# Unread products, seeds and a load moved in the start-up of a Fourier mixing and gated convolution kernel

## The chip, the cores and the metric

The kernel runs on one core of a Trainium2 chip. The metric is the device time of one execution in microseconds (us), as the median of several runs. A core has engines that run side by side, each with its own queue in program order: TensorE (PE, with PEld for its weight loads), VectorE (DVE), ScalarE (ACT), GpSimd (POOL) and SyncE (SP), which here only issues DMA transfers. ACT and POOL issue transfers too.

## The reference, cut to what matters

```python
X = np.fft.fft(x, axis=1)            # x: 8 x 3136 x 256, float32
x = np.fft.fft(X, axis=2).real
h = np.maximum(x @ w_in, 0.0)        # w_in: 256 x 1024, float64
conv_out = sum(conv_w[k] * hp[:, k:k + S, :] for k in range(3))   # hp: h with a row of zeros at both ends
gate = 1.0 / (1.0 + np.exp(-conv_out))
out = (h * gate) @ w_out             # w_out: 1024 x 256, float64
```

The weights come as float64; the kernel makes float32 of them with integer and float operations on DVE (`narrow`, L617).

## The kernel before, in words

The first transform runs along the 3136 rows. The kernel folds x by symmetry (`fold_ops`, L142, on DVE, with small copies on POOL and scalings on ACT), and multiplies the folds with tables of cosines and sines on PE (`units`, L344): an odd table `tab4` (loaded at L280, partly mirrored by ACT at L309) and an even one `tab2` (L260). The results are `pt` and `qt`, `PQ[b]` in the code. The second transform, along the 256 features, isn't done by itself: its matrix `dm` is multiplied once with w_in, which gives G (`blocks(i)`, L752, eight matmul records of 256 columns for quarter i of w_in, and two copies by ACT) and a short vector `ge` (`column(i)`, L763, eight records of one column). One feature needs extra care: a row `er` is put together on POOL (L454, L455) from `qt`'s last row, which a transfer fetches (L463), then stored and spread over all partitions (L470, L573).

Then come 256 steps (batch, chunk of rows, 128 of the 1024 columns of w_in), in a pipeline written out by hand at L1051:

- `seed` (L786, ACT) writes the share of `er` times `ge` into a PSUM bank `pa` (two such banks);
- `products` (L794, PE) makes `pb` from `qt` and G (one bank) and adds `pt` times G to `pa`;
- `copies` (L807, ACT) takes `pb` out, `combine` (L815, DVE) adds, subtracts and clips at zero, which gives h;
- `first_tap` (L821, ACT), `middle` (L825, an adding transfer from POOL) and `last_tap` (L830, DVE) are the convolution, `sigmoid` (L845) and `gate` (L853 POOL, L854 DVE) follow, and `mm2` multiplies with w_out five steps later.

Other work is hung into the steps with `at(cycle, place, function)`; within a step the places come in the order first, act, dve, pool, load, pe. A step uses 128 columns, so steps 0 and 1 need only the first quarter of w_in, steps 2 and 3 the second. The transform of the next batch is spread over the steps of this one. The order on each engine is that of the program; nothing is rearranged later.

Before the steps stands the start-up: load w_in's first quarter and x of batch 0 (two halves, `load_ops(0, 0)` and `load_ops(0, 1)`; each half is one load, L119, and four gathers issued by POOL, L132; the second half also has three loads of single rows, L126, issued by ACT), then make float32 of the taps and of w_in's first quarter (`w4[0]`, done by L654), fold the first half, `blocks(0)` and `column(0)`, fold the second half, and transform. `keep_on` (L892) issues products of the folds `w` that nobody reads: two before `blocks(0)`, two after `column(0)`. A product of 512 columns is two matmul records in the trace. The buffer of x's second half is reused by batch 1's first half, whose loads (`load_ops(1, 0)`) stand after the copy of `er`'s spread row (L948). w_in's second quarter is made float32 ahead of the seeds (its three parts: `power` on DVE and ACT, L631 and L633; `product`, L645 and L646; `value`, L639 and L654). `column(1)` and `blocks(1)` follow after step 0's products.

Of the kernel before, what the change touches and what calls it, by code (L numbers as in the profile page):

```python
# [9 lines left out]
F32 = mybir.dt.float32  # L10
# [27 lines left out]
def kernel(  # L38
# [10 lines left out]
    nc = tc.nc  # L49
    B, S, D = x.shape  # L50
    F = moe_w_in.shape[1]
    P = 128
    M = S // 2
    Q4 = S // 4
    NP = Q4 // NQ
# [26 lines left out]
    psa = ctx.enter_context(tc.tile_pool(name="psa", bufs=2, space=PSUM))  # L82
    psb = ctx.enter_context(tc.tile_pool(name="psb", bufs=1, space=PSUM))
# [8 lines left out]
    def mm(o, l, r, start, stop):  # L92
        nc.tensor.matmul(o, l, r, start=start, stop=stop, skip_group_check=True)  # L93

    def spare():

        return pso.tile([P, 2, D], F32, name="po", tag="po").rearrange("p a d -> p (a d)")
# [4 lines left out]
    xh, wt, ea = {}, {}, {}  # L102
# [7 lines left out]
    def load_ops(b, h, eng, other=None, held=False):  # L110


        def plain():
            t = xp.tile([P, 8, 2, D], F32, name="xh", tag="xh")
            xh[b, h] = t
            if held:

                nc.gpsimd.memset(t[0:1, 0, 0, 0:1], 0.0)
            eng.dma_start(out=t[0:NP, 0:4], in_=bass.AP(  # L119
                tensor=x.tensor, offset=x.offset + (b * S + 1 + 2 * h) * D,  # L120
                ap=[[HQ * D, NP], [Q4 * D, 4], [1, 2 * D]]))

        def zero():
            t = xh[b, h]
            for s0, n, r in ((0, 4, 0), (4, 3, 1), (7, 1, 0)):
                (other or eng).dma_start(out=t[NP:KR, s0:s0 + n], in_=bass.AP(  # L126
                    tensor=x.tensor, offset=x.offset + (b * S + r * Q4) * D,
                    ap=[[D, 1], [Q4 * D, n], [0, 2], [1, D]]))

        def mirrored(m):  # L130
            def f():
                nc.gpsimd.indirect_dma_start(  # L132
                    out=xh[b, h][0:NP, 7 - m].rearrange("p q d -> p (q d)"),
                    out_offset=None,
                    in_=bass.AP(tensor=x.tensor, offset=x.offset,
                                ap=[[2 * D, B * S // 2], [1, 2 * D]]),
                    in_offset=bass.IndirectOffsetOnAxis(ap=idx[0:NP, 0:1], axis=0),
                    element_offset=(b * S + (4 - m) * Q4 - HO + 2 * (1 - h)) * D)
            return f
        return [plain] + [zero] * h + [mirrored(m) for m in range(4)]  # L140
# [150 lines left out]
    def load_turn(eng):  # L291

        for s in range(2):
            for i in range(2):
                eng.dma_start(out=turn[i:NP:2, s].unsqueeze(2), in_=bass.AP(
                    tensor=dft_seq.tensor, offset=dft_seq.offset + ((2 + s) * NQ + HQ * i) * HE,
                    ap=[[4 * NQ * HE, NP // 2], [2 * HE, 2], [1, 1]]))

    def mend_row(par, half):

        for st in range(2):
            row = tabs[0][96:NP, st, HQ - 1] if par == 0 else tabs[1][96:NP, st, 1]
            act(row, row, AF.Copy, scale=half[96:NP])
# [353 lines left out]
    class Weight:  # L657
# [19 lines left out]
        def narrow(self, c0, c1):  # L677
# [13 lines left out]
    win = [pqp.tile([P, NK], F32, name="win", tag=tag)[:, 0:F].rearrange("p (i t n) -> p i t n", i=2, t=2)  # L691
           for tag in ("pt", "qt")]
# [5 lines left out]
    w4 = [win[i // 2][:, i % 2] for i in range(4)]  # L698
    raws = [None, None]

    def raw_in(i):
        def f(sh):
            if i % 2 == 0:
                raws[i // 2] = wp.tile([P, 2, *sh[1:]], I32, name="raw", tag="w%d" % (i // 2))
            return raws[i // 2][:, i % 2]
        return f

    w_in = [Weight(w4[i], moe_w_in[:, i * N4:(i + 1) * N4].rearrange("(t p) n -> p t n", p=P), raw_in(i))
            for i in range(4)]
# [17 lines left out]
    for f in load_ops(0, 0, nc.sync):  # L727
        f()
    load_turn(nc.scalar)
    for f in load_ops(0, 1, nc.sync, nc.scalar, True):  # L730
        f()

    act(first_use, low, AF.Sigmoid)
# [18 lines left out]
    def blocks(i):  # L752

        w = w4[i]
        for g in range(2):
            p = spare()
            for t in range(2):
                mm(p[:, 0:N4], dm[:, t, g, :], w[:, t], t == 0, t == 1)
            nc.scalar.copy(out=G[:, g, i * N4:(i + 1) * N4], in_=p[:, 0:N4])
        if i > 1:  # L760
            column(i)

    def column(i):  # L763

        w, p = w4[i], spare()
        for m in range(NF // 4):
            for t in range(2):
                mm(p[:, m:m + 1], w[:, t, m * P:(m + 1) * P], dm[:, t, 1, P - 1:P], t == 0, t == 1)
        nc.scalar.copy(out=ge[:, i * NF // 4:(i + 1) * NF // 4], in_=p[:, 0:NF // 4])
# [4 lines left out]
    hs, gs, pa, pb, po, nb = {}, {}, {}, {}, {}, {}  # L774

    def cut(s):
        b, c, f = s
        ch = chunks[c]
        return ch, ch.k1 - ch.k0, slice(f * P, (f + 1) * P)

    def seed(s):

        b, c, f = s
        ch, n, fs = cut(s)
        pa[s] = psa.tile([P, 512], F32, name="pa", tag="pa")
        act(pa[s][:, 0:n], eb[b, c], AF.Copy, scale=ge[:, f:f + 1])  # L786
# [7 lines left out]
    def products(s):  # L794
        b, c, f = s
        ch, n, fs = cut(s)
        pb[s] = psb.tile([P, 512], F32, name="pb", tag="pb")
        mm(pb[s][:, 0:n], G[0:P - 1, 1, fs], PQ[b][1][0:P - 1, ch.k0:ch.k1], True, True)
        mm(pa[s][:, 0:n], G[:, 0, fs], PQ[b][0][:, ch.k0:ch.k1], False, True)

    def copies(s):

        ch, n, fs = cut(s)
        p = pb.pop(s)
        nb[s] = nbp.tile([P, 2, HN], F32, name="nb", tag="nb")
        for i, cols in enumerate((ch.fcols, ch.cols)):
            act(nb[s][:, i, cols], p[:, cols], AF.Copy, scale=-1.0 if i else 1.0)  # L807
# [79 lines left out]
        gs.pop(s)  # L887


    idle = psb.tile([P, 512], F32, name="pb", tag="pb")  # L890

    def keep_on(banks):  # L892

        for p in banks:
            mm(p.rearrange("p (s q d) -> p s q d", s=2, q=2), wt[0][1][0:NP, 1, 0], wt[0][1][0:NP, 0:2, 0:2],
               True, True)

    begin, us, row, flip, store = units(0)
    begin()
# [3 lines left out]
    ops, _, pres = fold_ops(0)  # L903

    def folds(h):
        n = len(ops) // 2
        for j in range(n * h, n * h + n):
            if j in pres:
                pres[j]()
            ops[j]()  # L910
# [2 lines left out]
    w_out = Weight(wout, moe_w_out.rearrange("(c p) o -> p c o", p=P),  # L913
                   lambda sh: xp.tile(sh, I32, name="raw", tag="xh"))
    w_out.load(nc.sync)
    keep_on([idle] * 2)
    blocks(0)
    column(0)
    keep_on([psa.tile([P, 512], F32, name="pa", tag="pa") for _ in range(2)])
    mend_row(1, half)  # L920
    mirror_tables()
    folds(1)
    mend_row(0, half)
    for i in range(2):
        for u in odds:
            u.part(i)
# [17 lines left out]
    n = chunks[0].k1  # L944
    p = psd.tile([P, 512], F32, name="pd", tag="pd")
    mm(p[:, 0:n], one, er[0][:, 0:n], True, True)
    eb[0, 0] = ebp.tile([P, HN], F32, name="eb", tag="eb")[:, 0:n]
    nc.scalar.copy(out=eb[0, 0], in_=p[:, 0:n])  # L948
    for f in load_ops(1, 0, nc.sync):
        f()  # L950
    room = left[:, NF // 2:].rearrange("p f i -> p (f i)").bitcast(I32)
    for f in w_in[1].parts(0, 2, room):
        f()
    steps = [(b, c, f) for b in range(B) for c in range(len(chunks)) for f in range(NF)]
    per = len(chunks) * NF
    side = {}
# [2 lines left out]
    def at(cycle, where, fn):  # L959
        side.setdefault((cycle, where), []).append(fn)  # L960
# [2 lines left out]
        at((0, 0, 1, 3)[i], "pe", lambda i=i: blocks(i))  # L963

    early, *rest = w_in[2].parts(0, 2, room)
    for fn in rest:
        at(0, "dve", fn)
    for cycle, w_, c in ((1, w_in[3], 0), (3, w_out, 0), (5, w_out, 2), (7, w_out, 4), (9, w_out, 6)):
# [29 lines left out]
    for b in range(1, B):  # L998
# [4 lines left out]
        n = per * b - (2 if b == 1 else 3) - c0  # L1003
# [12 lines left out]
    for b in range(1, B):  # L1016
        ops, singles, pres = fold_ops(b)
        c0, n = ends[b - 1], ends[b] - ends[b - 1]
# [4 lines left out]
        else:  # L1023
            if b == 2:
                c0, n = c0 + 3, n - 3
# [16 lines left out]
    n = len(steps)  # L1042
    row_of(steps[0])
    seed(steps[0])
    seed(steps[1])
    products(steps[0])
    copies(steps[0])
    early()
    column(1)
    blocks(1)  # L1050
    for t in range(n + LAG):  # L1051
        def run(where):
            for fn in side.get((t, where), []):
# [97 lines left out]
```

## Time and profile before

| | us |
|---|---|
| median of 3 runs | 1169.77 (1169.37 to 1169.94) |
| profiled execution | 1170.58 |
| its span, first to last instruction | 1168.8 |
| PE busy | 1136.6 (97%) |
| DVE busy | 975.2 (83%) |
| ACT busy | 943.2 (81%) |
| POOL busy | 607.8 (52%) |

The mean granted TensorE clock of the span is 0.997. A row of the order of time gives the start, the length, the engine, the line of the kernel, the operation, what it writes and reads (partitions x elements), how many were merged, and in brackets how long the engine was idle before and what ended that. A product shows the line of its helper, L93; the tiles tell products apart: `pb<-w` and `pa<-w` the unread ones, `po<-win,dm` the blocks, `po<-dm,win` the column, `po<-tab,..` the transforms, `pd<-er,one` the spread of the row, `pb<-qt,G` and `pa<-pt,G` those of a step. A name with q, as SPq, is the engine's queue of DMA issues. A row of busy time by stretches gives from and to, the length, then for PE, PEld, DVE, ACT and POOL the busy time with the number of instructions, then the granted clock, the mean busy share of the 16 DMA engines and GB/s.

### The profile page before, as it was taken

What the parts mean: (1) busy time and instruction counts of PE and PEld (TensorE: products, weight loads), DVE (VectorE), ACT (ScalarE), POOL (GpSimd) and SP (SyncE); (2) the same over time, 40 slices, a digit from 0 to 9 for tenths busy, and PEclk for the clock granted to TensorE, in tenths of its full rate; (3) what the DMA queues carried; (4) which work ended last, traced back from release to release, by engine and by line L of the source; (5) the groups of instructions that cost most, each with busy time, mean ns of one, the idle gap of its engine ahead of it and who ended that gap; (6) DMA issues with size and microseconds to landing.
All of it is one profiled execution on the core that took longest, in us unless ns stands there. A gap on an engine that the chain in (4) does not pass through costs nothing.

```text
span 1168.8 us, 15881 instructions
## 1 busy us (share of the span) xinstructions
PE 1136.6 (97%) x4810; PEld 888.5 (76%) x4810; DVE 975.2 (83%) x1448; ACT 943.2 (81%) x1939; POOL 607.8 (52%) x738
## 2 busy tenths in 40 slices
PE   3999999999999999999999999999999999999998
PEld 2766787778777777777777777777778777777777
DVE  7699989998788879898887888879787778788885
ACT  2598878888788879888887888888887888898885
POOL 6256545656466464646455464655344344444443
PEclk9899999999999999999999999999999999999999
DMA  9677896776677676767675666855665656666654
GB/s 240 165 112 161 173 152 148 165 162 153 132 148 169 136 180 133 168 115 177 142 168 127 147 133 139 183 122 122 136 120 102 125 122 142 131 130 128 125 117 105
DMA packets 106200, 168.15 MB, mean 144 GB/s; under 512 B 31275, under 2 KB 61241, under 8 KB 106115
## 3 DMA queue, kind: packets, MB, share of 16 engines
q0 software_dynamic: 42160, 115.87, 51.7%
q1 hardware_dynamic: 63183, 51.11, 15.9%
q8 instruction: 38, 0.62, 0.2%
q14 instruction: 47, 0.39, 0.1%
q10 hardware_dynamic: 772, 0.16, 0.1%
HBM read 38.40 MB, written 25.74 MB: 55 GB/s over the span
## 4 chain that ended last, share of the span: by engine, by line
PE 79%; ACT 5%; DVE 4%; issue 2%; DMA 0%; DVEq 0%; ACTq 0%
PE po L93 49%; PE pb L93 12%; PE pa L93 12%; PE pd L93 6%; DVE g L830 1%; ACT nb L807 1%; ACT g L845 1%; ACT os L878 1%; ACT pa L786 0%; DVE g L854 0%; DMA out_dram<-os 0%; ACT g L821 0%; DVE h L815 0%; DVE xh L168 0%; DVE xh L157 0%
## 5 line engine op out<-in xcount | busy, mean ns | idle before, releaser
L93 PE MATMUL po<-wout,g 128*128 128x256 f32 x3072 | 706.7, 379 | 5.4 <-DVE g L854 4.7
L93 PEld LDWEIGHTS po<-wout,g 128*128 128x128 f32 x3072 | 580.4, 190 | 151.2 <-issue 19.5
L825 POOL DMA_DIRECT2D g<-h x256 | 228.0, 890 | 465.6 <-ACT g L821 291.8
L845 ACT ACTIVATE g<-g,cw 128x385 f32<-128x385 f32 (+2 forms) x512 | 292.4, 625 | 67.2 <-DVE g L830 66.2
L853 POOL TENSOR_TENSOR g<-g,h 128x385 f32<-128x385 f32 (+1 forms) x256 | 299.1, 1169 | 44.4 <-ACT g L845 42.8
L807 ACT ACTIVATE nb<-pb 128x386 f32<-128x386 f32 (+3 forms) x512 | 227.4, 499 | 110.0 <-PE pb L93 109.2
L815 DVE CUSTOM_DVE_ANT_0 h<-pa,nb 128x386 f32<-128x386 f32 (+3 forms) x512 | 264.4, 556 | 32.0 <-POOL h L792 19.3
L830 DVE SCALAR_TENSOR_TENSOR g<-h,cw,g 128x770 f32<-128x770 f32 (+1 forms) x256 | 282.5, 1104 | 0.0
L821 ACT ACTIVATE g<-h,cw 128x770 f32<-128x770 f32 (+1 forms) x256 | 244.6, 955 | 0.0
L93 PE MATMUL pb<-qt,G 127*128 127x387 f32 (+2 forms) x512 | 214.4, 500 | 1.8 <-ACT nb L807 1.8
L93 PE MATMUL pa<-pt,G 128*128 128x387 f32 (+2 forms) x512 | 212.0, 495 | 1.7 <-ACT pa L786 1.7
L854 DVE TENSOR_TENSOR g<-g,h 128x385 f32<-128x385 f32 (+1 forms) x256 | 190.1, 743 | 24.6 <-ACT g L845 24.5
L786 ACT ACTIVATE pa<-eb,ge 128x387 f32<-128x387 f32 (+2 forms) x256 | 155.5, 608 | 1.6 <-DVE h L815 1.2
L93 PEld LDWEIGHTS pa<-pt,G 128*128 128x128 f32 x512 | 96.9, 190 | 76.1 <-issue 18.2
L132 POOL DMA_INDIRECT xh<-in_x_dram,idx x64 | 90.5, 1413 | 19.4 <-issue 11.6
L93 PEld LDWEIGHTS pb<-qt,G 127*128 127x128 f32 x512 | 91.2, 191 | 9.4 <-ACT nb L807 4.0
L93 PE MATMUL pd<-tab,w 98*128 98x197 f32 (+2 forms) x448 | 97.7, 317 | 0.2 <-DVE as L419 0.2
L93 PEld LDWEIGHTS pd<-tab,w 98*128 98x128 f32 (+1 forms) x448 | 81.9, 191 | 9.5 <-ACT pa L786 0.6
L878 ACT COPY os<-po 128x256 f32<-128x256 f32 x196 | 57.4, 394 | 6.5 <-PE po L93 6.5
L168 DVE TENSOR_TENSOR xh<-xh 98x1024 f32<-98x1024 f32 (+1 forms) x32 | 48.7, 1522 | 0.1
L157 DVE TENSOR_TENSOR xh<-xh 98x1020 f32<-98x1020 f32 (+1 forms) x32 | 46.1, 1445 | 0.0
L392 DVE TENSOR_TENSOR as<-as,pd 128x196 f32<-128x196 f32 x14 | 5.0, 359 | 37.0 <-ACT as L388 37.0
(143 smaller groups left out, 452.9 us busy)
## 6 DMA issues: line engine op xcount, KB each, us to landing
g<-h POOLq DMA_DIRECT2D x192, 385.0 KB, 4.1
g<-h POOLq DMA_DIRECT2D x64, 416.0 KB, 4.2
out_dram<-os SPq DMA_DIRECT2D x96, 256.0 KB
xh<-in_x_dram SPq DMA_DIRECT2D x16, 784.0 KB
eb<-ed SPq DMA_DIRECT2D x16, 193.5 KB
raw<-in_moe_w_in_dram SPq DMA_DIRECT2D x4, 512.0 KB
raw<-in_moe_w_out_dram SPq DMA_DIRECT2D x1, 2048.0 KB
eb<-ed SPq DMA_DIRECT2D x8, 209.0 KB
```

The lines of the kernel that those rows point to most:

```text
L93: nc.tensor.matmul(o, l, r, start=start, stop=stop, skip_group_check=True)
L132: nc.gpsimd.indirect_dma_start(out=xh[b, h][0:NP, 7 - m].rearrange("p q d -> p (q d)"), out_offset=None, in_=bass.AP(tensor=x.tensor, offs ...
L786: act(pa[s][:, 0:n], eb[b, c], AF.Copy, scale=ge[:, f:f + 1])
L807: act(nb[s][:, i, cols], p[:, cols], AF.Copy, scale=-1.0 if i else 1.0)
L815: nc.vector._custom_dve(TENSOR_ADD_SAT, out=to, in0=a[:, cols], in1=c[:, i, cols], s0=BIG, s1=0.0)
L821: act(gs[s], hs[s][:, 0:n], AF.Copy, scale=cw[:, 0, s[2]:s[2] + 1])
L825: nc.gpsimd.dma_start(out=gs[s], in_=hs[s][:, 1:1 + n], accum_op=ALU.add)
L830: stt(out=g, in0=h[:, k:k + n], scalar=cw[:, k, f:f + 1], in1=g, op0=ALU.mult, op1=ALU.add)
L845: act(gs[s][:, c], gs[s][:, c], AF.Sigmoid, scale=cw[:, 1, s[2]:s[2] + 1])
L853: gt(g[:, p], g[:, p], h[:, p], op=ALU.mult)
L854: vt(g[:, v], g[:, v], h[:, v], op=ALU.mult)
L878: nc.scalar.copy(out=osb[:, j % 2], in_=pt[:, j % 2])
```

## The change

The three single-row loads of batch 0 go from ACT's queue to SP's. The unread products of the folds `w` are gone; in their place stand nine of w_in's first quarter with itself, ahead of all folds: one into each `pa` bank, seven into `pb`. Batch 1's first half of x is loaded right after the folds of batch 0, ahead of its transform. The seeds of steps 0 and 1 go ahead of the second quarter's float32 parts, and `column(1)` and `blocks(1)` go into step 0's place "first", which is behind step 1's products and copies. On ACT that puts the two seeds ahead of L633, and step 1's copies ahead of the column's and blocks' copies. On POOL the four gathers stand ahead of L454, on SP the load ahead of L470.

```diff
-    for f in load_ops(0, 1, nc.sync, nc.scalar, True):
+    for f in load_ops(0, 1, nc.sync, None, True):
         f()
...
-    idle = psb.tile([P, 512], F32, name="pb", tag="pb")
-
-    def keep_on(banks):
-
-        for p in banks:
-            mm(p.rearrange("p (s q d) -> p s q d", s=2, q=2), wt[0][1][0:NP, 1, 0], wt[0][1][0:NP, 0:2, 0:2],
-               True, True)
+    for pool, tag, n in ((psa, "pa", 1), (psa, "pa", 1), (psb, "pb", 7)):
+        p = pool.tile([P, 512], F32, name=tag, tag=tag)
+        for _ in range(n):
+            mm(p, w4[0][:, 0, 0:P], win[0][:, 0].rearrange("p t n -> p (t n)"), True, True)
...
     w_out.load(nc.sync)
-    keep_on([idle] * 2)
     blocks(0)
     column(0)
-    keep_on([psa.tile([P, 512], F32, name="pa", tag="pa") for _ in range(2)])
     mend_row(1, half)
     mirror_tables()
     folds(1)
     mend_row(0, half)
+    for f in load_ops(1, 0, nc.sync):
+        f()
...
-    for f in load_ops(1, 0, nc.sync):
-        f()
     room = left[:, NF // 2:].rearrange("p f i -> p (f i)").bitcast(I32)
-    for f in w_in[1].parts(0, 2, room):
-        f()
...
+    at(0, "first", lambda: column(1))
+    at(0, "first", lambda: blocks(1))
...
     seed(steps[0])
     seed(steps[1])
+    for f in w_in[1].parts(0, 2, room):
+        f()
     products(steps[0])
     copies(steps[0])
     early()
-    column(1)
-    blocks(1)
```

## The prediction

> **What bounds the kernel now.** I read the page first, then the busy time by stretches, then the order of time in the first 60 us.
>
> ```profile
> span 1168.8 us, 15881 instructions
> ## 1 busy us (share of the span) xinstructions
> PE 1136.6 (97%) x4810; PEld 888.5 (76%) x4810; DVE 975.2 (83%) x1448; ACT 943.2 (81%) x1939; POOL 607.8 (52%) x738
> ```
> ```profile
> 0.00:20.00 20.00, 1.10 (x3) 1.00 (x4) 14.11 (x29) 1.66 (x4) 15.71 (x33) 1.00 0.90 225
> 20.00:45.00 25.00, 24.54 (x124) 18.71 (x122) 18.66 (x36) 12.47 (x32) 8.66 (x14) 1.00 0.68 205
> ...
> 70.00:100.00 30.00, 27.66 (x112) 20.63 (x111) 29.79 (x47) 24.85 (x52) 13.84 (x24) 1.00 0.60 117
> ...
> 150.00:200.00 50.00, 50.00 (x228) 39.83 (x227) 44.14 (x74) 37.69 (x78) 24.75 (x31) 1.00 0.78 157
> ```
>
> In the second answer the first bracketed pair after a stretch's length is PE, then weight loads, DVE, ACT, POOL; then the granted clock, DMA share and GB/s. PE is the bound: 50.00 of 50.00 us in 150 to 200. Of its 32.2 idle us (1168.8 - 1136.6), 18.9 lie before 20. In 70 to 100 DVE is full (29.79 of 30) and PE is not. So whatever brings all three engines to step 2 earlier is kept to the end; PE alone early is worth nothing. No part of the change reaches past about 60 us, except by that shift.
>
> **Part 1: the first 29 us.**
>
> ```profile
> 6.26 0.97 POOL L132 DMA_INDIRECT xh<-in_x_dram,idx  x1 [0.30 <-issue]
> ...
> 8.67 0.69 DVE L654 SCALAR_TENSOR_TENSOR win<-raw,win 128x512 f32<-128x512 f32 x1
> ...
> 11.50 0.17 DVE L717 TENSOR_TENSOR small<-cw 128x8 f32<-128x8 f32 x1 [2.14 <-ACT cw L715]
> ...
> 12.51 2.34 DVE L157 TENSOR_TENSOR xh<-xh 98x1020 f32<-98x1020 f32 x2
> ...
> 17.70 1.22 SPq L260 DMA_DIRECT2D tab<-dft_seq_dram  x2
> ...
> 19.49 3.78 PE L93 MATMUL pb<-w 98*128 98x512 f32 x4 [13.42 <-POOL w L179]
> ...
> 23.06 3.33 PE L93 MATMUL po<-win,dm 128*128 128x256 f32 x8
> ...
> 26.23 0.95 PE L93 MATMUL po<-dm,win 128*128 128x1 f32 x8
> ...
> 27.04 1.96 PE L93 MATMUL pa<-w 98*128 98x512 f32 x4
> ...
> 28.23 1.20 ACT L309 ACTIVATE tab<-tab 99x196 f32<-99x196 f32 x4
> ...
> 29.17 0.86 PE L93 MATMUL po<-tab,h 98*128 98x197 f32 x4
> ...
> 29.40 0.66 POOL L202 COPY ea<-xh 99x4 f32<-99x4 f32 x1
> ```
> ```profile
> xh<-in_x_dram,idx POOLq DMA_INDIRECT x1, 6.0
> ```
> ```profile
> SPq L670 <- DMA dm<-dft_dim_dram: 0.9, 1, 0.9
> ```
> ```profile
> tab<-dft_seq_dram SPq DMA_DIRECT2D x2, 589.5 KB
> ```
> ```profile
> DMA packets 175, 0.91 MB, mean 226 GB/s; under 512 B 24, under 2 KB 32, under 8 KB 175
> ```
> ```profile
> DMA packets 1173, 2.32 MB, mean 387 GB/s; under 512 B 39, under 2 KB 39, under 8 KB 1173
> ```
>
> The last two rows are all DMA from 20 to 24 and from 27 to 33.
>
> *The three row loads off ACT.* DVE's wait of 2.14 us for ACT goes. The second fold needs the fourth gather (issued 6.26, landing 6.0 later: 12.26); it began at 12.51 + 1.17 = 13.7. So the folds gain 1.3 of the 2.1 us: done at about 28.8, not 30.1. SP takes the three loads while it waits for the dm memset anyway: nothing. But the loads deal out their completion slots anew: the fourth odd-table load now shares one with the second half of x, which landed at 17.70 (what held L260 until then). L260 goes out about 0.6 us later.
>
> *The unread products.* Eighteen records start at 9.4 (end of L654) instead of four at 19.49 and four at 27.04. A record takes 0.945 us (3.78/4) on the slow clock, 0.49 (1.96/4) on the full one. In the trace the slow clock lasts from 19.49 to about 26.0, 6.5 us of work. So seven records are slow and eleven fast, and with the overlap that the starts show (0.86 and 0.43 apart) they end near 20.5. dm is there by 19.84 (it held SP's L670). Blocks and column of the first quarter then run on the full clock: half of 3.33 plus some overlap lost, 1.8, and 0.95, to about 23.3 instead of 27.2. ACT copies and mirrors the odd table (0.8 + 1.20 us) by about 25.5.
>
> *What is late next.* The first long products read the even table. Its 1.18 MB (2 x 589.5 KB) move from 20 on in packets of 5.2 KB on average (0.91 MB/175); by 27 the packets are the weights' 2 KB. At 226 GB/s that is 5.2 us: landed at 25.2 to 26; with the 0.6 us, I take 26.1. Bounds: 25.2 (no delay) and 29.17 (it was there when first read). So PE starts them at 26.1 instead of 29.17: **-3.1 us**, between -4.0 and 0. Between 23.7 and 26.1 PE has no work: the products on w that filled this place are gone.
>
> **The clock in that gap.**
>
> ```profile
> 43.03:46.44 3.41, 2.21 (x6) 0.63 (x5) 3.34 (x7) 2.43 (x5) 2.59 (x3) 1.00 0.59 129
> 87.40:90.81 3.41, 1.92 (x8) 0.97 (x7) 3.41 (x5) 1.29 (x3) 0.87 (x1) 1.00 0.74 136
> ```
> ```profile
> 46.40:46.50 0.10, 0.10 (x1) 0.00 (x0) 0.10 (x1) 0.10 (x1) 0.10 (x1) 0.74 0.12 46
> ...
> 53.20:53.30 0.10, 0.10 (x1) 0.02 (x1) 0.00 (x0) 0.00 (x0) 0.00 (x0) 0.62 0.58 164
> ```
>
> The last row but one has the clock fall at 46.45, the last has it back at 53.28: 6.83 us at half speed. I look at half of that, 3.41 us, before the fall: PE was busy 2.21, of which some 0.66 was a product of one row. At 87.40 to 90.81 it was busy 1.92 with full products and the clock stayed. So the line lies near 1.55 to 1.92 full us in 3.41. A 3.41 us stretch that ends at 26.1 would hold 0.4 us of table product and about 0.6 of column: below the line. I expect the clock to fall near 26 and to stay half for another 6.8 us, in which PE does 3.4 us of work too little: **+3.4 us** (bounds: 0 if it stays, 1.7 if it is back after one such half, 3.4). DVE and ACT wait for PE here (the transforms), so it is paid in full.
>
> The Trainium skill (TensorE: Matmul & The Clock Gate, Part 1) says that the clock halves after about one idle window of some 3.4 us and advises against PE gaps beyond about 3 us. By that rule a 2.4 us gap would cost nothing; this trace's fall at 46.45, after a longest gap of 1.2 us, does not agree with it.
>
> **Part 2: from the one-row product to step 2.**
>
> ```profile
> 42.78 0.91 PE L93 MATMUL pd<-er,one 1*128 1x386 f32 x2
> ...
> 44.49 0.72 ACT L633 ACTIVATE win<-win,low 128x512 int32<-128x512 int32 x1 [0.28 <-DVE win L631]
> ...
> 45.12 1.07 ACT L786 ACTIVATE pa<-eb,ge 128x386 f32<-128x386 f32 x2
> ...
> 45.74 0.99 PE L93 MATMUL pa<-pt,G 128*128 128x386 f32 x2 [1.20 <-ACT pa L786]
> ...
> 46.13 0.85 ACT L807 ACTIVATE nb<-pb 128x385 f32<-128x385 f32 x2
> ...
> 46.98 1.84 PE L93 MATMUL po<-dm,win 128*128 128x1 f32 x8 [0.25 <-DVE win L654]
> ...
> 48.68 3.76 PE L93 MATMUL po<-win,dm 128*128 128x256 f32 x8
> ...
> 54.37 0.59 ACT L786 ACTIVATE pa<-eb,ge 128x386 f32<-128x386 f32 x1
> 54.39 1.02 DVE L815 CUSTOM_DVE_ANT_0 h<-pa,nb 128x385 f32<-128x385 f32 x2 [3.39 <-PE pa L93]
> ```
>
> All times here are on the axis of before; part 1's shift comes on top. Now the seeds go ahead of L633: they start at 44.2 and PE's second product at 44.8, so its gap shrinks from 1.20 to about 0.3. ACT does the same work in all, so its copies still end near 46.7 to 46.9. Step 1's two products follow at once (there is one pb bank, freed by these copies): to 48.4. Then column and blocks, 0.95 and 1.9 at full clock, to about 50.9; G's last copy 51.3; step 2's seed at 51.3 to 51.5 instead of 54.37. DVE makes the second quarter about 0.6 later (its L639 waits for L633), which PE meets only at 48.4; its wait of 3.39 us at step 1 goes. From the seed on the three engines follow one another as before: **-2.9 us**, of which 2.8 is the slow column and blocks (1.84 + 3.76, halved). It needs the full clock. PE's weakest 3.41 us now hold 1.75 full us (gaps of 0.3 and 1.3, the one-row product), just inside what the rows above leave open. If the clock falls here too, column and blocks come after step 1's slow products and the seed is at about 54.9: 0.
>
> **Batch 1's x earlier.**
>
> ```profile
> 37.46 0.70 ACTq L463 DMA_DIRECT2D er<-qt  x1
> ...
> 39.49 0.54 POOL L454 TENSOR_TENSOR er<-as 1x197 f32<-1x197 f32 x1 [9.44 <-DMA er<-qt]
> ...
> 41.85 1.09 POOL L132 DMA_INDIRECT xh<-in_x_dram,idx  x1 [0.20 <-POOL er L455]
> ```
>
> The buffer of this x is free when the folds end (28.8), so its four gathers and one load run from there instead of from 41.85. POOL, idle then, is done by 34. Queued behind them are POOL's four operations on the row er (L454 on) and SP's store of er with the three spreads of it; SP and POOL hold nothing else there. In before er crosses idle queues in 2.0 us. It now meets the rest of 1.6 MB of x (the load and four gathers of 98 x 2 KB). PE's one-row product comes 1.1 us after POOL's last operation on the row (41.85 - 0.20, to 42.78), so I take 0, bounds 0 and +3.2 (er behind all of x: 28.8 to 41.8 at 225 GB/s after the weights, then 2.0).
>
> **Sum.** -3.1 + 3.4 - 2.9 = -2.6. The profiled execution took 1170.58 (span 1168.8 and 1.8 around it), which gives 1168.0; the timed runs' median, 1169.77, lies 0.8 under the profiled one, so I predict 1167.2.
>
> **Rivals and chances** (0.2%, some 2.3 us, is about what a measurement of this kernel can tell from no change).
> - Forecast, gap slows PE, step 2 early: 1167.2, chance 0.30.
> - The clock stays in the gap, so -3.1 - 2.9: 1163.8, chance 0.17. For it: dense work at 87.40 survived 1.92. The skill's rule above is this case. With the clock back after half of 6.83 us: 1165.5, chance 0.20.
> - The clock falls at the second place, so the reorder does not do what it says: with the gap slow as well 1170.1 (+0.3), chance 0.14; without, or with half of it, 1166.8 to 1168.4, chance 0.12. For it: 1.75 is close to the line.
> - Slower: er is held by x. It decides from a landing more than 1.1 us late. At its bound PE stands 3.2 us, which also drops the clock: +0.3 + 3.2 = 1173.3, chance 0.07. Against it: the row is on ACT's queue, x on SP's and POOL's.
>
> Those under 1167.4 (0.17 + 0.20, over half of the first and part of the mixed case) give faster 0.58; same 0.31; slower 0.11, as the last has smaller forms. The range reaches from 1163.8 to 1170.4 and leaves out the slow end and the lowest tail.
>
> **What would show it.** Unread products ending near 20.5; column ending near 23.3; PE idle to about 26.1 and then 0.86 us groups of table products taking twice that; the clock at 0.50 from near 26 to 33 and 1.00 from 43 to 55; step 2's seed 8.5 us after the one-row product begins (42.8 to 51.3), where it was 11.6 (42.78 to 54.37). Wrong if the even table lands later than 27, if the clock shows no fall near 26, or if L454 starts more than 3.5 us after L463.

## The result and the profile after

| | before | after |
|---|---|---|
| median of 22 runs each, side by side, us | 1169.16 (1166.87 to 1170.57) | 1171.99 (1168.04 to 1173.44) |
| ratio, 95% interval | | 1.002 (1.0012 to 1.0028) |
| profiled execution, us | 1170.58 | 1169.80 |
| its span, us | 1168.8 | 1168.0 |
| mean granted clock | 0.997 | 0.995 |

The changed kernel is slower by 0.2%, some 2.8 us by the medians; 1167.2 was forecast. Of its 22 runs 7 lie at 1168.0 to 1170.0 with a mean clock of 0.994 to 0.997, and 15 at 1171.4 to 1173.4 with 0.992 or 0.993: the first profile is of the smaller group, so the account of the loss goes by another execution of the same kernel, e9_after_look, at 1171.97.

The page of after, its first lines:

```profile
span 1168.0 us, 15898 instructions
...
PE 1141.3 (98%) x4820; PEld 891.2 (76%) x4820; DVE 975.7 (84%) x1448; ACT 942.2 (81%) x1939; POOL 608.9 (52%) x738
```

Busy time of after by the stretches shown of before (PE, weight loads, DVE, ACT, POOL, then clock, DMA share, GB/s), and four slices of 0.1 us that show where the clock changes:

```profile
0.00:20.00 20.00, 11.12 (x23) 5.25 (x24) 15.60 (x32) 1.75 (x4) 16.50 (x33) 1.00 0.89 228
20.00:45.00 25.00, 19.15 (x113) 16.76 (x111) 15.87 (x32) 11.01 (x30) 10.79 (x17) 0.91 0.86 254
45.00:60.00 15.00, 14.01 (x50) 8.64 (x49) 11.47 (x23) 11.01 (x25) 2.31 (x4) 0.81 0.67 85
...
70.00:100.00 30.00, 27.62 (x112) 20.64 (x111) 29.79 (x48) 24.77 (x53) 13.86 (x23) 1.00 0.60 117
...
26.80:26.90 0.10, 0.10 (x1) 0.10 (x2) 0.10 (x1) 0.10 (x1) 0.00 (x0) 0.92 1.12 410
...
30.20:30.30 0.10, 0.10 (x2) 0.10 (x1) 0.00 (x0) 0.00 (x0) 0.00 (x1) 0.52 1.00 369
...
43.90:44.00 0.10, 0.10 (x1) 0.10 (x2) 0.04 (x1) 0.00 (x0) 0.10 (x1) 0.76 0.00 0
...
50.80:50.90 0.10, 0.10 (x1) 0.00 (x0) 0.10 (x1) 0.10 (x1) 0.00 (x0) 1.00 0.20 56
```

From 70 on the two kernels read alike, as the forecast said; the whole difference lies in the first 60 us. PE has 10 us more of busy time before 20 (the unread products), and less of it from 20 to 45. A mean clock of 0.91 and 0.81 in the last two early stretches stands for two spells at half speed: the slices put them at 26.88 to 30.30 and 43.95 to 50.78. They last 3.41 and 6.83 us, and 13.65 us lie between them: one, two and four times 3.41. So it is in every profile here: the changes of the clock lie on a grid of 3.41 us, and where the grid lies differs from execution to execution.

The order of time of after, with the steps that the forecast names:

```profile
11.27 1.92 PE L93 MATMUL pa<-win 128*128 128x512 f32 x2
12.97 6.30 PE L93 MATMUL pb<-win 128*128 128x512 f32 x14
19.35 1.97 PE L93 MATMUL po<-win,dm 128*128 128x256 f32 x8
21.15 0.95 PE L93 MATMUL po<-dm,win 128*128 128x1 f32 x8
...
26.76 1.53 PE L93 MATMUL po<-tab,h 98*128 98x197 f32 x4 [4.22 <-ACT h L218]
...
28.32 0.34 SPq L119 DMA_DIRECT2D xh<-in_x_dram  x1
...
36.74 0.76 ACTq L463 DMA_DIRECT2D er<-qt  x1
...
42.00 0.94 ACT L467 ACTIVATE er<-er 1x392 f32<-1x392 f32 x1 [2.72 <-DMA er<-qt]
42.10 0.57 DVE L374 TENSOR_TENSOR qt<-as,po 128x393 f32<-128x393 f32 x1 [2.16 <-DMA er<-qt]
42.12 0.54 POOL L454 TENSOR_TENSOR er<-as 1x197 f32<-1x197 f32 x1 [8.08 <-DMA er<-qt]
...
43.75 1.49 PE L93 MATMUL pd<-er,one 1*128 1x386 f32 x2 [1.63 <-POOL er L454]
...
54.02 0.59 ACT L786 ACTIVATE pa<-eb,ge 128x386 f32<-128x386 f32 x1
```

The brackets carry the finding. Four engines stand until the row `er` has landed: ACT 2.72 us, DVE 2.16, POOL 8.08, and through POOL PE 1.63. The row is issued at 36.74, earlier than before (37.46), and POOL can use it only at 42.12: 5.4 us, where before took 2.0. The first answer to why it is late is in the transfers of after, from 36 to 42.2, then a queue's row of 39 to 40 and one of 40 to 41:

```profile
DMA packets 623, 1.30 MB, mean 210 GB/s; under 512 B 85, under 2 KB 85, under 8 KB 621
...
q0 software_dynamic: 48, 0.12, 40.2%
...
q10 hardware_dynamic: 3, 0.00, 1.7%
```

q1 is SP's queue (x's load), q0 POOL's (x's gathers), q10 ACT's, with the row's six packets. In 36 to 42.2, x's two queues move 1.27 of 1.30 MB. q10 moves nothing until 40.5: q0 is then all but done (48 packets from 39 to 40, 5 from 40 to 41). The row, on a third queue, came when x was nearly through.

The same steps in e9_after_look, an execution at the median of after:

```profile
37.74 0.76 ACTq L463 DMA_DIRECT2D er<-qt  x1
...
42.02 0.53 POOL L454 TENSOR_TENSOR er<-as 1x197 f32<-1x197 f32 x1 [8.01 <-DMA er<-qt]
...
43.65 0.91 PE L93 MATMUL pd<-er,one 1*128 1x386 f32 x2 [0.54 <-POOL er L454]
...
50.39 1.71 PE L93 MATMUL po<-dm,win 128*128 128x1 f32 x8
51.96 3.76 PE L93 MATMUL po<-win,dm 128*128 128x256 f32 x8
...
56.02 0.59 ACT L786 ACTIVATE pa<-eb,ge 128x386 f32<-128x386 f32 x1
```

Here the forecast can be settled term by term. The row is issued at 37.74, 0.28 behind the 37.46 of before, and -3.1 + 3.4 was +0.3. That it fits so closely is luck: the three executions of after issue it at 36.74, 37.74 and 39.65. Then the row costs 4.28 us instead of 2.03, that is 2.25 more, of which PE has 1.66 to spare (its one-row product came 42.78 - 39.49 = 3.29 us after POOL's start in before and can come 43.65 - 42.02 = 1.63 after it), so that PE stands 0.54 (2.25 - 1.66 = 0.59). Last, from PE's one-row product to step 2's seed are 12.4 us, not the 8.5 forecast: 3.9 more, the slow clock's: column and blocks take 1.71 and 3.76 us instead of 0.95 and 1.97, and the products of step 1 ahead of them are slow as well. Together the seed is at 56.02, some 4.3 us behind the forecast 51.7 and 1.65 behind the 54.37 of before.

### The profile page after: what moved, and what is told of

Its sections match the earlier page's. It is cut to its first block, busy times and chain, and to the rows that moved or that the text cites. A ratio compares the mean times of both kernels' runs of the same rounds, so it can differ in the third digit from the quotient of the medians.

```text
span 1168.0 us, 15898 instructions
## 1 busy us (share of the span) xinstructions
PE 1141.3 (98%) x4820; PEld 891.2 (76%) x4820; DVE 975.7 (84%) x1448; ACT 942.2 (81%) x1939; POOL 608.9 (52%) x738
## 4 chain that ended last, share of the span: by engine, by line
PE 79%; ACT 5%; DVE 4%; issue 2%; DMA 0%; DVEq 0%; ACTq 0%
PE po L93 49%; PE pb L93 12%; PE pa L93 12%; PE pd L93 6%; DVE g L830 1%; ACT g L845 1%; ACT nb L807 1%; ACT os L878 1%; ACT pa L786 0%; ACT g L821 0%; DVE h L815 0%; DVE g L854 0%; DMA out_dram<-os 0%; DVE xh L157 0%; DVE xh L173 0%
## 5 line engine op out<-in xcount | busy, mean ns | idle before, releaser
L93 PEld LDWEIGHTS po<-wout,g 128*128 128x128 f32 x3072 | 581.5, 190 | 149.8 <-issue 19.3
L815 DVE CUSTOM_DVE_ANT_0 h<-pa,nb 128x386 f32<-128x386 f32 (+3 forms) x512 | 264.5, 557 | 29.1 <-POOL h L792 20.4
L132 POOL DMA_INDIRECT xh<-in_x_dram,idx x64 | 93.8, 1466 | 20.1 <-issue 11.3
```

Source lines behind the costliest of these rows:

```text
L132: nc.gpsimd.indirect_dma_start(out=xh[b, h][0:NP, 7 - m].rearrange("p q d -> p (q d)"), out_offset=None, in_=bass.AP(tensor=x.tensor, offs ...
L815: nc.vector._custom_dve(TENSOR_ADD_SAT, out=to, in0=a[:, cols], in1=c[:, i, cols], s0=BIG, s1=0.0)
```

## The experiments

Two accounts were put against each other. In one, x ahead of the row holds `er`, and by this wait the clock falls the second time. In the other, the slow clock of the gap after the column is what costs. Each kernel has its own median of before from the same chip: 1169.13 for the first four, 1169.05 for e5 to e8, 1169.62 for the rest.

| run | what | median us | ratio to before (95%) | L463 to L454, us | seed of step 2 at |
|---|---|---|---|---|---|
| e1_x_back | after, x at its old place | 1168.05 | 0.9998 (0.9989 to 1.0006) | 2.1 | 50.99 |
| e2_x_early_only | before, x early | 1171.77 | 1.0031 (1.0021 to 1.0041) | 6.8 | 55.58 |
| e3_seeds_only | before, part 2's order | 1167.20 | 0.9985 (0.9977 to 0.9994) | 2.1 | 49.84 |
| e4_fill_gap | after, gap filled | 1169.64 | 1.0006 (0.9997 to 1.0014) | 7.0 | 52.89 |
| e5_x_back_fill | e1 and e4 | 1165.22 | 0.9966 (0.9952 to 0.9979) | 2.1 | 48.72 |
| e6_rows_on_act | after, rows on ACT | 1169.77 | 1.0007 (0.9997 to 1.0016) | 4.5 | 53.21 |
| e7_load_early | after, gathers at the old place | 1166.95 | 0.9983 (0.9974 to 0.9992) | 2.1 | 51.30 |
| e8_gathers_early | after, load at the old place | 1166.85 | 0.9980 (0.9971 to 0.9989) | 2.1 | 51.41 |
| e10_products_seeds | e1, rows on ACT | 1168.36 | 0.9992 (0.9983 to 1.0001) | 2.0 | 51.19 |

### e1_x_back: x at its old place

```diff
     mend_row(0, half)
-    for f in load_ops(1, 0, nc.sync):
-        f()
...
     nc.scalar.copy(out=eb[0, 0], in_=p[:, 0:n])
+    for f in load_ops(1, 0, nc.sync):
+        f()
     room = left[:, NF // 2:].rearrange("p f i -> p (f i)").bitcast(I32)
```

> The changed kernel with batch 1's x back behind the spread of the row er, where it was. Theory 1 (er's fetch is held by that x; in the trace of the changed kernel L454 starts 5.4 us after L463 instead of 2.0, PE stands 1.6 us and the clock falls a second time): L454 again about 2.0 us after L463, no PE wait at the one-row product, 2 to 5 us faster than the changed kernel, 1167 to 1170. Theory 2 (the loss is the clock in the gap between column and even table alone): within 1 us of the changed kernel, about 1172, with the same fall near 26.

1168.05 us. The order of time, and the stretch of 3.4 us behind the row in which PE has least to do:

```profile
37.19 0.76 ACTq L463 DMA_DIRECT2D er<-qt  x1
39.27 0.54 POOL L454 TENSOR_TENSOR er<-as 1x197 f32<-1x197 f32 x1 [10.81 <-DMA er<-qt]
...
50.99 0.59 ACT L786 ACTIVATE pa<-eb,ge 128x386 f32<-128x386 f32 x1
```
```profile
44.00:47.40 3.40, 2.06 (x6) 0.93 (x6) 2.66 (x5) 2.45 (x5) 2.79 (x5) 1.00 0.63 153
```

The row takes 2.1 us again, the second fall is gone, and the seed is 5.0 us ahead of e9's, as the first theory expected. From 36 to 42 nothing but the row and an instruction fetch crosses (7 packets, 0.01 MB). The first fall is still there (24.4 to 31.2), and this kernel only equals before: what the fall costs takes up what part 1 and part 2 bring.

### e2_x_early_only: x early and nothing else, in before

```diff
     mend_row(0, half)
+    for f in load_ops(1, 0, nc.sync):
+        f()
...
     nc.scalar.copy(out=eb[0, 0], in_=p[:, 0:n])
-    for f in load_ops(1, 0, nc.sync):
-        f()
```

> The kernel before with batch 1's x alone moved behind the folds. Theory 1: er lands 3 us or more late, PE waits 1 to 3 us for it, 1 to 4 us slower than before, 1170 to 1173. Theory 2: x costs nothing, within 0.5 us of before.

```profile
27.61 0.86 PE L93 MATMUL po<-tab,h 98*128 98x197 f32 x4
...
35.90 0.70 ACTq L463 DMA_DIRECT2D er<-qt  x1
...
42.73 0.54 POOL L454 TENSOR_TENSOR er<-as 1x197 f32<-1x197 f32 x1 [7.07 <-DMA er<-qt]
...
44.37 1.65 PE L93 MATMUL pd<-er,one 1*128 1x386 f32 x2 [3.08 <-POOL er L454]
```

1171.77 us: this one move alone is as slow as the whole change. PE's wait of 3.08 us agrees with the 1.66 to spare (6.8 - 2.0 - 1.66 = 3.1), and the one-row product runs at half speed (1.65 us): the clock is down from 43.4 to 53.7. The row is used 0.6 us later than in after though it was issued 0.8 earlier; x's gathers are issued 1.6 us later here (from 30.75, in after from 29.13), so the landing goes with x and not with the row's own issue.

The first row shows something else. Up to the folds this is the code of before, and yet its table products begin at 27.61 and not at 29.17: its blocks take 1.92 us, in before's profile 3.33, because the clock of the start came up earlier. In e3, with the same start, it is 1.97 and 27.71. So before's profile, by which part 1 was measured, was some 1.5 us later at this place than two other executions of the same code.

### e3_seeds_only: part 2's order and nothing else, in before

```diff
-    for f in w_in[1].parts(0, 2, room):
-        f()
...
+    at(0, "first", lambda: column(1))
+    at(0, "first", lambda: blocks(1))
...
     seed(steps[1])
+    for f in w_in[1].parts(0, 2, room):
+        f()
...
     early()
-    column(1)
-    blocks(1)
```

> The kernel before with the seeds and step 1's products alone moved ahead of the second quarter. As predicted: 2.9 us faster, 1166.3, if the clock stays up between 43 and 55; about 0 if it falls there in spite of the order.

```profile
41.34 0.91 PE L93 MATMUL pd<-er,one 1*128 1x386 f32 x2
...
46.75 0.95 PE L93 MATMUL po<-dm,win 128*128 128x1 f32 x8
47.56 1.97 PE L93 MATMUL po<-win,dm 128*128 128x256 f32 x8
...
49.84 0.59 ACT L786 ACTIVATE pa<-eb,ge 128x386 f32<-128x386 f32 x1
```

1167.20 us. From product to seed are 8.5 us, the number forecast, with column and blocks at 0.95 and 1.97: no clock falls. Part 2 by itself is worth 0.15%, some 1.8 us, less than the 2.9 forecast.

### e4_fill_gap: the gap filled, x still early

```diff
     column(0)
+    for _ in range(4):
+        mm(p, w4[0][:, 0, 0:P], win[0][:, 0].rearrange("p t n -> p (t n)"), True, True)
```

The four (eight records) are read by nothing.

> The changed kernel with four more unread products (eight records) behind the first quarter's column, into the gap ahead of the even table. Theory 1: the clock stays up there, but er's landing is set by x's transfers (41 to 42), so within 1 us of the changed kernel. Theory 2: 1.7 to 3.4 us faster, 1168.5 to 1170.

```profile
26.27 0.86 PE L93 MATMUL po<-tab,h 98*128 98x197 f32 x4
...
34.57 0.76 ACTq L463 DMA_DIRECT2D er<-qt  x1
...
41.57 0.53 POOL L454 TENSOR_TENSOR er<-as 1x197 f32<-1x197 f32 x1 [7.37 <-DMA er<-qt]
...
43.20 1.65 PE L93 MATMUL pd<-er,one 1*128 1x386 f32 x2 [3.26 <-POOL er L454]
```

The first fall is gone: four table products take 0.86 us, not 1.53. The row is issued 3.2 us ahead of e9's, and PE's one-row product begins only 0.45 ahead: the wait for the row took the rest. The kernel is at 1169.64, some 2.4 us under after's median: the time lies in the range of the second theory, the late row is that of the first. The gap costs too, though not by the path that the forecast had: the second spell at half speed is shorter here (42.1 to 48.9, against 46.2 to 56.5 in e9).

### e5_x_back_fill: both

The edits of e1 and e4.

> The changed kernel with batch 1's x back behind the row er and four more unread products in the gap ahead of the even table. If the late row and the fall of the clock in the gap are the two losses and add up: the clock never falls, the even table's products start at 26.3, step 2's seed near 48.5, 3 us or more faster than the changed kernel with x back alone (1168.05), 1163.5 to 1165.5. If the two losses are one and the same: no better than 1167.

```profile
26.55 0.93 PE L93 MATMUL po<-tab,h 98*128 98x197 f32 x4 [0.56 <-DMA tab<-dft_seq_dram]
...
37.00 0.54 POOL L454 TENSOR_TENSOR er<-as 1x197 f32<-1x197 f32 x1 [8.69 <-DMA er<-qt]
...
40.22 0.91 PE L93 MATMUL pd<-er,one 1*128 1x386 f32 x2
...
48.72 0.59 ACT L786 ACTIVATE pa<-eb,ge 128x386 f32<-128x386 f32 x1
```
```profile
20.00:45.00 25.00, 23.11 (x128) 17.72 (x127) 18.84 (x37) 14.14 (x36) 11.01 (x17) 1.00 0.71 216
45.00:60.00 15.00, 14.23 (x67) 10.28 (x65) 12.49 (x25) 13.18 (x30) 4.26 (x8) 1.00 1.09 189
```

1165.22 us (1165.05 to 1165.67), under both kernels: in the range expected if the two losses add up, though 2.8 and not 3 us under e1. The clock is 1.00 all the way; from product to seed are 8.5 us again. With x back, filling the gap brings the product 2.3 us forward (42.49 in e1 to 40.22), where with x early it brought 0.45.

### e6_rows_on_act: the three row loads back on ACT's queue

```diff
-    for f in load_ops(0, 1, nc.sync, None, True):
+    for f in load_ops(0, 1, nc.sync, nc.scalar, True):
```

> The changed kernel with the three single-row loads back on ACT's queue. If they only hurry the folds, which PE does not wait for: within 0.5 us of the changed kernel, 1171.5 to 1172.5. If their place also moves the even table (slots dealt out anew): its products start up to 0.6 us earlier and the time is up to 1 us less. If the earlier folds are what lets x start and reach er: 1 us or more less.

The stretch from 46.04 in e6:

```profile
46.04:49.45 3.41, 3.12 (x5) 1.36 (x6) 2.79 (x6) 2.34 (x5) 0.00 (x0) 0.51 0.41 134
```

1169.77 us, 2.2 under after's median. The third expectation has such a time, but by a row that is less late, and that is not so: the row still takes 4.5 us and PE waits 0.79. What differs is that the second spell lasts one stretch of 3.4 us (46.1 to 49.5), so that the column runs at full speed (0.95). Only 1 of its 11 runs has after's clock of 0.992. e10 tests whether the rows matter by themselves.

### e7_load_early and e8_gathers_early: one half of x each

In e7 only the load stays early, in e8 only the four gathers; the other half goes to the old place.

```diff
-    for f in load_ops(1, 0, nc.sync):
-        f()
+    x10 = load_ops(1, 0, nc.sync)
+    x10[0]()
...
+    for f in x10[1:]:
+        f()
     room = left[:, NF // 2:].rearrange("p f i -> p (f i)").bitcast(I32)
```

In e8 `x10[0]()` and the loop change places, and the tile of x is taken ahead of the gathers.

> The changed kernel with x's one load early and its four gathers back behind er. If the load on SP's queue holds er: L454 3 us or more after L463, close to the changed kernel. If the gathers do: L454 2.0 to 2.5 us after L463, as fast as with all of x back (1168.05). If it takes both, by the sum of bytes: 2.5 to 3.5 us after, between the two.

> The changed kernel with x's four gathers early and its load back behind er's spread. If the gathers hold er: L454 3 us or more after L463, close to the changed kernel (1172). If the load does: 2.0 to 2.5 us after, as fast as with all of x back (1168.05). If it takes both: between.

The order of time of e7, and its transfers from 36 to 41:

```profile
37.48 0.76 ACTq L463 DMA_DIRECT2D er<-qt  x1
...
39.60 0.53 POOL L454 TENSOR_TENSOR er<-as 1x197 f32<-1x197 f32 x1 [11.16 <-DMA er<-qt]
```
```profile
DMA packets 233, 0.46 MB, mean 93 GB/s; under 512 B 17, under 2 KB 17, under 8 KB 231
```

Neither half holds the row: 2.1 us in both, no second fall, 1166.95 and 1166.85 us. This does not single out a queue. A half is over before the row comes: in e7 its last packets pass by 38.0, in e8 (0.52 MB) by 38.75, and the row's after 38.75 and 39.0. What the two show is that `er` is not held once x is through. The six profiles in which it is held say a little more: when the row's first packet passes, at most 0.04 MB of the gathers are left, but in e4 still 0.18 MB of the load. So the row is not behind all of the load; that the gathers' queue holds it would fit, but was not tested. That e7 and e8 are both some 1.1 us under e1, with the same clock, was not followed up.

### e9_after_look, e9_after_look_b: the unchanged kernel again

> The changed kernel as it is, for a second profile: 15 of its 22 runs had a mean clock of 0.992 (1171.4 to 1173.4), the profiled one 0.995 (1169.8). If the dear runs fall in the gap for 6.8 us and again at the late row for longer: a cold stretch from near 24 to 31 and one from near 41 to 51, span near 1170. If they lose the clock at a third place: a cold stretch after 55.

> The same kernel once more, since one look may fall on the rarer kind of run: as for the look before.

1171.97 and 1174.04 us, both with a clock of 0.992. The first is shown above. Three of its stretches, the one at whose end the clock falls (at 46.2) and the two behind it:

```profile
42.90:46.31 3.41, 2.53 (x8) 0.89 (x6) 3.18 (x8) 1.80 (x5) 1.33 (x5) 0.99 0.01 4
46.31:49.72 3.41, 2.74 (x5) 1.18 (x4) 2.80 (x6) 2.34 (x5) 0.00 (x0) 0.50 0.53 185
49.72:53.14 3.42, 3.42 (x13) 2.90 (x12) 3.35 (x7) 0.67 (x3) 0.00 (x0) 0.50 0.50 51
```

The spells are 25.7 to 32.6 and 46.2 to 56.5, 17.1 us or five stretches of 3.41, against 10.2 or three in the first profile; in the second execution 28.1 to 34.9 and 48.5 to 58.8, five again. That is the first of the two expectations, some 2 and 5 us later than it had them. A slow stretch takes 3.41 x 0.5 / 1168 = 0.0015 off the mean clock, and so five go with 0.992 and three with 0.995: the two groups of runs of after differ by two slow stretches, 3.4 us, and their medians by 2.9. What brings the clock back is not the share of PE's work alone: it came back after the stretch of e6 with 3.12 busy us and after one of 3.41 in after (26.88 to 30.30), and did not after one of 3.16 in before (46.45 to 49.86) or after the last one above, which was full.

### e10_products_seeds: parts 1 and 2 without the rows and without x

The edits of e1 and e6.

> The changed kernel with x back and the three row loads back on ACT: of the four parts only the early unread products and the reorder of seeds and step 1 are left. If the row loads matter only through the time at which x starts (with x early they cost 2.2 us): the same as with x alone back, 1168.05 within 0.5. If they matter by themselves: 1166 or less. The fall of the clock in the gap near 25 stays in both cases.

1168.36 us, 0.3 from e1's 1168.05, with the same single spell (24.8 to 31.6) and the seed at 51.19 against 50.99. Where x is back, it makes no difference on which queue the rows are. So what they do in e6 they do together with x, whose load goes out at 30.09 there instead of 28.32; how that shortens the second spell stays open.

## Why the prediction was wrong

**The step that failed: "Batch 1's x earlier", taken at 0.** Its bound of +3.2 had the mechanism (the row behind all of x), and the rival "er is held by x" had its price, 1173.3; it got 0.07 because "the row is on ACT's queue, x on SP's and POOL's". That reason does not hold here: q10 stood while q0 and q1 worked. In the six profiles with all of x early the row is used at 42.1 (after), 42.0 and 44.1 (the two of e9), 42.7 (e2), 41.6 (e4) and 42.3 (e6), 4.3 to 7.0 us after its issue; in those without, 2.0 to 2.1 us after it. That the move is what costs is shown from both sides: taken back it brings 0.22% (e1), made alone it costs 0.31% (e2). The forecast's own sign, L454 more than 3.5 us after L463, is what came (5.4). In e9 PE's direct loss is small, 0.54 us, and most of the price is the second fall. Where PE gets to the row earlier, in e2 and e4, its direct wait is the larger part (3.08 and 3.26 us).

**The second fall, given 0.14 with a slow gap.** All six profiles with all of x early show it (after, both e9, e2, e4, e6), and none of the six with part 2's order and the row on time (e1, e3, e5, e7, e8, e10). Before has the row on time and falls too, in its own order. So in the new order the fall goes with the row's delay and not with the reorder, which the forecast feared. In e9 it costs 3.9 us. The forecast's line (1.55 to 1.92 full us of work in 3.41) holds: e9 fell after 2.53 busy us, 0.84 of them the one-row product, which leaves 1.69, and e1 and e3 stayed up, whose thinnest stretch, the one-row product left out, holds 1.83 wherever it is laid (1.75 forecast). Laid on the grid of 3.41 us, all 15 falls (those at the kernels' very end aside) come after a stretch with at most 1.79 us of PE's work, the one-row product left out, and no stretch at full speed with 1.80 or more ended in one. That is a reading of these profiles after the fact; no run was made to test it.

**Part 1, -3.1: too large, and by other terms.** The table products begin at 26.76 in after, 26.46 and 28.03 in the two of e9 (26.1 forecast). Against the 29.17 of before's profile the first is -2.4; against the 27.61 and 27.71 of e2 and e3, which have before's code up to there, it is some -0.9. The forecast read one execution and took its late clock for a trait of the kernel. The unread products begin at 11.3 (9.4 forecast) and end at 19.3 in after and 20.4 in e9 (20.5): all but the first two run on the full clock in after (6.30 / 14 = 0.45 us each), some more on the slow one in e9 (7.44). The column ends at 22.1 and 22.9 (23.3). The even table's load is issued at 17.50 in after and 17.34 in e9, not 0.6 us behind the 17.70 of before, and in both the wait of the table products ends, by the profile, with ACT's scaling of the folds (L218) and not with the table.

**The gap, +3.4: right.** The clock falls at 26.9 in after and at 25.7 in e9; the spell is 3.4 us in the first, the half-spell bound, and 6.8 in the second, as forecast. The gap itself is 4.22 and 3.10 us, not 2.4, as the column ends earlier. So the rule that the forecast set aside (the Trainium skill, TensorE: Matmul & The Clock Gate, Part 1: one idle window of about 3.4 us) is met in after, and the trace agrees with it: of the 3.41 us ahead of the fall PE was busy 0.13. In e9 it was busy 1.02 of them, so the window was not an idle one, and the clock fell all the same. At the second place the rule is not met either: PE's waits ahead of that fall are 0.54 and 0.35 us in e9. Filled, the gap shows no fall (e4, e5).

**Part 2, -2.9: right in its mechanism.** 8.5 us from product to seed in e3, e1 and e5. In the profiles that is 3.1 us (8.5 against the 11.6 of before), in the ratio of e3 some 1.8. Not every run of before has the fall that part 2 removes: of the 31 beside e3, 6 ran at a clock of 0.999 or 1.000 and took 1165.3 to 1168.6. As e3's thinnest stretch holds 1.83 us and before's 1.44, depending on where the grid lies, it would fit that before falls in some executions and e3 in none; the rest of the difference was not followed up.

**The rest.** From 70 on nothing changed. Seeds and products alone (e10, e1) give about before's time; x early is the 0.22% on top, some 2.6 us (from a ratio of 0.9998 to 1.002); the gap is worth 2.8 once x is back (1168.05 to 1165.22; by the ratios 3.7).

**Open.** Why the second spell lasts 3.4 us (e6), 6.8 (first profile, e4) or 10.2 (e9, e2), and why the one-row product should not count as work. Whether a single queue, still busy at the row's turn, would hold it: in e7 and e8 it was done. Getting the row to POOL by another way with x early was not tried.

## What to carry to other kernels

Before a bulk transfer is moved forward, list the small transfers that become due while it is under way, on whatever queue, and put the end of the bulk at their landing: here 6 KB waited until 0.6 to 1.6 MB had passed. A wait of half a microsecond on the engine that sets the pace cost 3.9 us more through the clock in e9, so price its spell and not its length. Where the clock moves, take a start time from more than one execution: before's profile was some 1.5 us later at the table products than two others with the same code. Where early work leaves a hole, the work and the hole are one change: e5 shows that the same parts pay 0.34% once the hole is filled and the bulk is put back.

## What the runs showed of the hardware

- A 6.1 KB transfer on a queue of its own took 4.3 to 7.0 us from issue to use instead of 2.0 to 2.1 while two other queues moved 0.6 to 1.6 MB. The Trainium skill (DMA: Bandwidth & Descriptors, Queues, rings and completion order) says that a DMA engine takes the queues that have work in turn, a packet at a time; by that the row should wait for a packet or so of each of the others. The trace shows q10's first packet some 2.5 us later than in e1, counted from the issue (3.9 us in after, 1.4 in e1); what held it inside an engine no run here shows.
- All changes of the granted clock in a profile lie on a grid of 3.41 us, so that the spells at half speed lasted 3.41, 6.83 or 10.24 us; the grid lies elsewhere in each execution.
- The clock fell in stretches in which PE was busy 2.2 to 2.5 of 3.4 us, with no wait above 1.2 us (before, e9), where a part of that work was a product of one row. A spell ended after a stretch of 3.12 busy us (e6) and went on after a full one (e9).
- A run's mean clock counts its slow stretches: in the profiles two go with 0.996 or 0.997, three with 0.995 or 0.996, five with 0.992, none with 1.000.
